# Folding halves spread over a group's second layer, and norms moved to ScalarE, in a fused retention, expert and channel kernel

## The chip, the cores and the metric

The kernel runs as one program on one core of a Trainium2 chip. The metric is the device time of one execution in microseconds. The engines are TensorE (PE, with its weight loads as PEld), VectorE (DVE), ScalarE (ACT), GpSimd (POOL) and SyncE (SP), which issues nearly all DMA transfers in one queue. "us" is microseconds throughout.

## The reference

Three stages follow each other on 4 batches of 576 rows of 512 values:

```python
ret = scores * Dmat; x = ret @ v                       # retention, 8 heads
h = np.maximum(x[b, s] @ w1[e], 0.0)                   # one expert of 8 for each row
out[b, s] = p[e] * (h @ w2[e])
X = np.real(fft(fft(x, axis=1), axis=2)); u = x + X    # third stage
un = (u - mean(u)) / np.sqrt(var(u) + 1e-06)
y = u + np.maximum(un @ w_ch1, 0.0) @ w_ch2            # 512 -> 2048 -> 512
```

The change touches the third stage alone: the transform of a batch, its norm, and the order in which a batch's steps stand among the products of the two layers.

## The kernel before

The third stage is in `Transform` (one batch's Fourier transform, sums and norm) and `channels` (the two layers). The order of all its instructions is that of the code: each engine takes its own in that order, and waits for semaphores where another engine's result is needed.

**A batch's transform.** `steps(b, wait)` is a generator. One `next` issues one step: `load` (DMAs into `fxy`), the folds of three row tiles (`even` makes `fee`, `odd` makes `foo`, both on VectorE), `twice` (four sums on VectorE), five products `down` on TensorE, each with `take` (ScalarE copies PSUM to `fz`), three cross products `across` with `merge` (ScalarE and VectorE) and `sums` (ScalarE), and then `end`: `rate`, and six times `norm` and `keep`. A norm makes r*x + m as fp32 rows `f`, the fp16 part `h` and the rest `l` = f - h, and stores h and l to `un` in DRAM; `keep` stores u. Both go through SyncE's queue. `h` and `l` are halves of a tile `hl`, of which there are three, so a fourth norm needs the first one's store to have ended; `f` lies in buffers that the folds use too, two for each half of the tiles.

**The two layers.** Batch 0 and 1 are prepared before and during the first 512 rows. The other rows go in seven groups of 256 rows, j = 0 to 6. `fetch(r)` loads a group's rows of `un`, transposed, into `gxt`. The first layer has eight slots f; in each, TensorE makes 24 products into a bank `g1` (L1666), ScalarE takes the two middle parts out (L1975, L1976), VectorE makes `s` from all four (L1982), and both make the fp16 parts `hd` of it (L1955, L1952). The second layer has seven products i (L2011), each 24 matmuls into a bank, and VectorE folds each into the rows `u` (L2040). Of the seven, the banks are

```python
q, tag = (p2, "g2") if i % 3 else (p1, "g1")
```

with three buffers `g1` and two `g2`, so the product i = 4 needs the bank of i = 1, and i = 5 that of i = 2.

**Where the steps stand.** Batch 2 (the third) has `more = tr.steps(2, 0)`, batch 3 `tr.steps(3, WAIT)` with WAIT = 1. In j = 0, `next(more)` is called after each of the seven products of the second layer. In j = 1 to 3 it is called once in every slot of the first layer too, and in j = 1 again in the slots of the table `TWICE` (1 and 4 before). At i = 4 of j = 1 what is left of `more` is issued, and then the fetch for j = 2 stands in SyncE's queue behind the last norm's stores. Beside them runs `left`, which combines pairs of weight pieces (`pair` loaded by SyncE, L1813; VectorE L1843 and L1848; ScalarE L1819; VectorE L1821) for the second layer's corner products; it ends in i = 2 of j = 0. Batch 1's norms stand among the products before j = 0, and the fetch for j = 0 and the rest of the pair loads stand behind their stores in SyncE's queue.

Of the kernel before, what the change touches and what calls it, by code (L numbers as in the profile page):

```python
# [14 lines left out]
ACTF = mybir.ActivationFunctionType  # L15
ALU = mybir.AluOpType
# [1180 lines left out]
def by_rows(nc, out, in_):  # L1197

    n = out.shape[0]
    m = n // 16 * 16 if n > 96 else n  # L1200
    for a, b in ((0, m), (m, n)):
        if a < b:
            i = nc.sync.dma_start(out=out[a:b], in_=in_[a:b])  # L1203
    return i


class Transform:
# [143 lines left out]
    def both(self, b, t, bank):  # L1351

        nc, n, (_, _, cd, sd) = self.nc, 34 if t == 2 else 128, self.tables
        zs = self.rows_of(b, t)
        out = []
        for s in (self.minus, sd):
            ps = bank()
            even, odd = ps[:n, 0:129], ps[:n, 129:257]
            steps = (
                (even, zs[0], 128, cd[:, 0, 0:129]),  # L1360
                (even, zs[2], 96, cd[:, 1, 0:129]),
                (odd, zs[1], 128, cd[:, 0, 129:257]),
                (even[:, 0:128], zs[3], 128, s[:, 0, :]),
                (odd, zs[4], 128, s[:, 1, :]),
            )
            for j, (o, z, m, w) in enumerate(steps):
                nc.tensor.matmul(
                    out=o, lhsT=z[:m], rhs=w[:m], start=(j == 0), stop=(j == 4)
                )
            out.append(ps)  # L1370
        return out
# [144 lines left out]
    def norm(self, b, i, kept=0):  # L1516

        nc, (_, _, _, r, m) = self.nc, self.st[b]
        t, y, p0, p1, at = self.place(b, i)
        n = TL[t][1]  # L1520
        x = self.xy[b][t][:n, y]
        f = self.wk.tile([128, 512], FP32, tag="xo" if y else "xe", name="f", bufs=2)
        hl = self.wk.tile([128, 2, 512], FP16, tag="hl", name="hl", bufs=3)
        h, l = hl[:n, 0, :], hl[:n, 1, :]
        ri, mi = r[:n, i : i + 1], m[:n, i : i + 1]
        nc.scalar.activation(out=h, in_=x, func=ACTF.Identity, scale=ri, bias=mi)
        nc.vector.tensor_scalar(out=f[:n], in0=x, scalar1=ri, scalar2=mi, op0=ALU.mult, op1=ALU.add)  # L1527
        nc.vector.tensor_tensor(out=l, in0=f[:n], in1=h, op=ALU.subtract)
        p0 = max(p0, kept)
        if p0 < p1:  # L1530
            to = slice(at.stop - (p1 - p0), at.stop)
            by_rows(nc, self.un[to, :], hl[p0:p1].rearrange("p a d -> p (a d)"))
        return hl
# [15 lines left out]
    def steps(self, b, wait=0):  # L1549

        self.load(b)
        yield
        for t in range(3):
            self.even(b, t)
            if wait:
                yield
            self.odd(b, t)
            yield
        self.twice(b, 0)
        self.twice(b, 1)  # L1560
        yield
        for _ in range(wait):
            yield
        yield from self.across_rows(b)
# [16 lines left out]
def channels(ctx, tc, nc, A, w1, w2, un, u, out, tr, wst, idn, late, jobs):  # L1581
# [47 lines left out]
    def still(n, ps):  # L1629

        for _ in range(n):
            nc.tensor.matmul(out=ps, lhsT=w1.dst[0][:, 0, 0:128], rhs=w1.dst[0][:, 0, 0:512], start=True, stop=True)
# [28 lines left out]
    def first(f, ps, xt, steps=range(3)):  # L1661

        for i in steps:
            m, x = ((h1, 0), (l1, 0), (h1, 1))[i]
            for k in range(4):
                nc.tensor.matmul(  # L1666
                    out=ps,
                    lhsT=m[:, k + 4 * (f // 8), 128 * (f % 8) : 128 * (f % 8) + 128],
                    rhs=xt[x][:, k, :],
                    start=(k == 0 and i == 0),  # L1670
                    stop=(k == 3 and i == 2),
                )
# [180 lines left out]
    ready = {}  # L1853
    E = {}
    OLD = 2
    TWICE = 1, 4
    WAIT = 1
    LEFT = 6
    DOWNS = 10
# [4 lines left out]
    def old(r, n):  # L1864

        x = wst.tile([128, 2, 512], FP32, tag="wst", name="u")
        nc.sync.dma_start(out=x, in_=u[r : r + 256, :].rearrange("(a p) d -> p a d", p=128))  # L1867
        return x
# [28 lines left out]
    for _ in left:  # L1897
        pass
    V.scalar_tensor_tensor(
        out=fs[:, 0:1], in0=w1.inv[:, 0:1], scalar=2.0**-10 / C2, in1=w2.inv[:, 0:1], op0=ALU.mult, op1=ALU.mult  # L1900
# [7 lines left out]
    for t in range(4):  # L1908
        ps = p2.tile([128, 512], FP32, tag="g2", name="g2")
        for at, f in enumerate(ROWS):  # L1910
            for i, (m, x) in enumerate(((h2, 0), (h2, 1), (l2, 0))):
                nc.tensor.matmul(
                    out=ps,
# [29 lines left out]
    for r0 in range(512, NT, 256):  # L1943
        xt = X.pop(r0)
        xt = xt[:, 0:4], xt[:, 4:8]
        j = (r0 - 512) // 256
# [4 lines left out]
        def lower(l, x, h):  # L1951
            V.scalar_tensor_tensor(out=l, in0=x, scalar=C2 / 2, in1=h, op0=ALU.mult, op1=ALU.subtract)  # L1952

        def whole(s, hd):
            nc.scalar.activation(out=hd[:, 0, 2:7], in_=s, func=ACTF.Copy, scale=C2 / 2)  # L1955
            lower(hd[:, 1, 2:7], s, hd[:, 0, 2:7])

        s = None
        for f in range(8):
            if f == OLD:  # L1960
                o = old(r0, 256)

            ps = p1.tile([128, 512], FP32, tag="g1", name="g1")
            if j == f == 0:
                still(STILL[2], ps)
            first(f + 8, ps[:, 0:256], xt)
            first(f, ps[:, 256:512], xt)
            old_s, old_hd = s, f and hd
            if f and f < 7:
                whole(s, hd)  # L1970
            r = wk.tile([128, 2, 128], FP32, tag="r", name="r")
            s = wk.tile([128, 640], FP32, tag="s", name="s").rearrange("p (a n) -> p a n", a=5)
            hd = hp.tile([128, 2, 7, 128], FP16, tag="hd", name="hd")
            p = ps.rearrange("p (a n) -> p a n", a=4)
            nc.scalar.activation(out=r, in_=p[:, 1:3], func=ACTF.Relu)  # L1975
            nc.scalar.activation(out=hd[:, 0, 0:2], in_=p[:, 1:3], func=ACTF.Relu, scale=C2 / 2)  # L1976
            for d, x, y, op in (
                (s[:, 1:3], p[:, 0:4:3], r[:, 1::-1], ALU.add),
                (s[:, 3:5], p[:, 0:4:3], r, ALU.subtract),
                (s[:, 0], p[:, 1], r[:, 1], ALU.add),  # L1980
            ):
                V.scalar_tensor_tensor(out=d, in0=x, scalar=0.0, in1=y, op0=ALU.max, op1=op)  # L1982
            if f == 7:
                whole(old_s, old_hd)
            lower(hd[:, 1, 0:2], r, hd[:, 0, 0:2])
            hid.append(hd)
            if j:
                next(more, None)
            if j == 1 and f in TWICE:
                next(more, None)  # L1990
            if j or f < LEFT:
                next(left, None)
# [34 lines left out]
        for i, (x, w, to) in enumerate(steps):  # L2027
            ps = banks[i] if i < 3 else place(i)
            product(ps, range(6 if i < 3 else 0, 8), x, w)
            next(more, None)  # L2030
            next(left, None)
            if i == 4 and r0 + 256 < NT:
                if j in (1, 3):
                    for _ in more:
                        pass
                fetch(r0 + 256)
            for a, c in to:
                y = q[:, a]
                p = ps.unsqueeze(1).to_broadcast([128, 2, 256]) if isinstance(a, slice) else ps
                V.scalar_tensor_tensor(out=y, in0=p, scalar=fs[:, c : c + 1], in1=y, op0=ALU.mult, op1=ALU.add)  # L2040
            if i == 4 and j:
                store(r0, o[:, 0])
# [175 lines left out]
def fused_kernel(tc, A, out, stop=None):  # L2218
    nc = tc.nc
    with ExitStack() as ctx:  # L2220
# [5 lines left out]
        with tc.manual_schedule():  # L2226
# [121 lines left out]
            z = zeros(cv)  # L2348
            steps = moe(ctx, tc, nc, A, xs, x2, rows_in, rows_out, pieces, weights, who, conv, low, start, beyond, z, padded, hid0, mt0, wst, small)
            next(steps)  # L2350
            for t, n in zip(tables, ("f_cs", "f_sn", "f_cd", "f_sd")):
                nc.sync.dma_start(out=t.rearrange("p a b -> p (a b)"), in_=A[n])
        overflow(tc, nc, A, xs, x2, idn, n_i)
        with tc.manual_schedule():
            late = next(steps)
            c2x.close()
            tr = Transform(ctx, tc, nc, x2, un, u, rows_out, tables)
            channels(ctx, tc, nc, A, c1, c2, un, u, out, tr, wst, idn, late, jobs)
# [46 lines left out]
```

## Time and profile before

| what | value |
|---|---|
| median of 3 runs | 793.76 us (791.66 to 795.1) |
| the profiled execution: its own time | 787.88 us |
| its span, first to last instruction | 785.7 us |
| TensorE matmul busy, share of the span | 724.8 us, 92% |
| VectorE busy | 592.3 us, 75% |
| ScalarE busy | 411.8 us, 52% |
| mean granted TensorE clock | 0.988 of full speed |
| first product of the first layer, j = 0 and j = 1 | at 470.87 and 520.11 us |
| the same of j = 2 | at 570.13 us |

A time of the profile counts from the span's start. A share of busy time says little about a single stage, so the sections below go by the timeline of the stretch from 440 to 660 us, in which the steps that the change moves lie.

### The profile page before, as it was taken

How to read it: one execution, taken by the hardware profiler on the slowest of the kernel's cores; microseconds unless marked ns; L12 is line 12 of the kernel's file. 1: busy time of each engine (PE TensorE's matmuls, PEld its weight loads, DVE VectorE, ACT ScalarE, POOL GpSimd, SP SyncE). 2: the span in 40 equal slices, each digit the busy share in tenths (PEclk: the TensorE clock that was granted, in tenths of full speed). 3: DMA queues.
4: the chain of work that ended last, by engine and by line, in shares of the span. 5: the costliest groups of instructions: out<-in, count | busy, mean ns of one | idle time of the engine just before them, and what ended most of it. 6: DMA issues, size and time to landing. Idle time of an engine off the chain costs nothing. (4 is left out here: it accounts for less than half of the span.)

```text
span 785.7 us, 17150 instructions
## 1 busy us (share of the span) xinstructions
PE 724.8 (92%) x6529; PEld 542.8 (69%) x6529; DVE 592.3 (75%) x1432; ACT 411.8 (52%) x829; POOL 126.8 (16%) x225
## 2 busy tenths in 40 slices
PE   8888898899999998879998999899899999999996
PEld 5677685655566555557644448778788888888885
DVE  3678888589889988857898969958876695646462
ACT  1356657378888797845847526426332451414140
POOL 3566443002102201113000011010010001010101
PEclk9999999899999999999999999999999999999998
DMA  9998449999998998964427276600550017110000
GB/s 296 355 305 293 154 115 309 295 315 344 293 360 304 270 352 287 262 235 149 136 77 240 102 214 232 175 28 2 170 150 2 28 62 195 28 55 2 28 2 27
DMA packets 91929, 142.27 MB, mean 181 GB/s; under 512 B 48116, under 2 KB 49017, under 8 KB 90814
## 3 DMA queue, kind: packets, MB, share of 16 engines
q1 hardware_dynamic: 87246, 126.78, 51.4%
q0 software_dynamic: 4592, 14.31, 5.0%
q8 instruction: 53, 0.87, 0.4%
q14 instruction: 38, 0.31, 0.1%
HBM read 97.55 MB, written 35.12 MB: 169 GB/s over the span
## 5 line engine op out<-in xcount | busy, mean ns | idle before, releaser
L1666 PE MATMUL g<-gxt,wh 128*128 128x256 f16 (+1 forms) x992 | 143.6, 284 | 2.6 <-DMA gxt<-un 1.4
L2011 PEld LDWEIGHTS <-hd 128*128 128x128 f16 x1176 | 114.2, 98 | 26.9 <-issue 7.1
L1666 PEld LDWEIGHTS <-wh 128*128 128x128 f16 x1056 | 102.8, 98 | 28.5 <-issue 4.9
L286 DVE SCALAR_TENSOR_TENSOR wl<-wst,ws,wh 128x1024 f16<-128x1024 f32 (+1 forms) x82 | 100.3, 1253 | 8.1 <-ACT wh L281 8.0
L281 ACT ACTIVATE wh<-wst,ws 128x1024 f16<-128x1024 f32 x80 | 89.0, 1140 | 26.1 <-DVE ws L274 25.7
L815 PE MATMUL ps<-xt,wh 128*128 128x320 f16 (+4 forms) x544 | 79.1, 284 | 8.1 <-DMA xt<-xs 5.8
L845 PE MATMUL ps<-wh,hid 128*128 128x512 f16 (+2 forms) x528 | 84.6, 302 | 0.2 <-ACT hid L831 0.2
L2011 PE MATMUL g<-wh,hd 128*128 128x256 f16 x448 | 78.3, 273 | 4.3 <-DVE u L2040 2.0
L1666 PE MATMUL g<-gxt,wl 128*128 128x256 f16 (+1 forms) x496 | 80.5, 285 | 0.0
L815 PEld LDWEIGHTS <-wh 128*128 128x128 f16 x640 | 57.5, 100 | 33.2 <-issue 13.8
L1872 POOL DMA_INDIRECT out<-u,orow x18 | 17.9, 993 | 383.9 <-DVE u L2040 284.8
L845 PEld LDWEIGHTS <-hid 128*128 128x128 f16 (+2 forms) x792 | 46.4, 100 | 42.4 <-issue 2.7
L239 ACT ACTIVATE wh<-wst 128x1024 bf16<-128x1024 f32 x66 | 69.3, 1050 | 7.7 <-DVE wst L311 5.2
L2040 DVE SCALAR_TENSOR_TENSOR u<-g,ffs,u 128x256 f32<-128x256 f32 (+1 forms) x63 | 34.1, 568 | 49.3 <-PE g L2011 48.7
L1982 DVE SCALAR_TENSOR_TENSOR s<-g,r 128x256 f32<-128x256 f32 x168 | 53.3, 374 | 23.4 <-ACT hd L1976 22.7
L1955 ACT ACTIVATE hd<-s 128x640 f16<-128x640 f32 x56 | 41.3, 737 | 47.8 <-DVE s L1982 47.8
L1975 ACT ACTIVATE r<-g 128x256 f32<-128x256 f32 x56 | 21.1, 378 | 84.0 <-PE g L1666 78.0
L2011 PE MATMUL g<-e,hd 128*128 128x256 f16 x504 | 59.9, 273 | 5.0 <-DVE u L2040 4.0
L859 POOL DMA_INDIRECT x<-y,mt x25 | 31.5, 1261 | 194.7 <-ACT y L857 149.7
L2011 PE MATMUL g<-wl,hd 128*128 128x256 f16 x224 | 61.1, 273 | 0.0
L1666 PEld LDWEIGHTS <-wl 128*128 128x128 f16 x528 | 51.9, 98 | 11.7 <-issue 1.1
L845 PE MATMUL ps<-wl,hid 128*128 128x512 f16 (+2 forms) x264 | 56.4, 302 | 0.0
(299 smaller groups left out, 1280.7 us busy)
## 6 DMA issues: line engine op xcount, KB each, us to landing
wst<-in_moe_w SPq DMA_DIRECT2D x64, 512.0 KB
raw<-in_ch SPq DMA_DIRECT2D x14, 1024.0 KB
qk<-in_qkv SPq DMA_DIRECT2D x18, 512.0 KB
vk<-in_qkv SPq DMA_DIRECT2D x16, 512.0 KB
pair<-ch SPq DMA_DIRECT2D x32, 256.0 KB
ch<-d SPq DMA_DIRECT2D x14, 512.0 KB
wst<-ch SPq DMA_DIRECT2D x14, 512.0 KB
u<-u SPq DMA_DIRECT2D x9, 512.0 KB
```

The costliest lines, as they stand in the source:

```text
L239: self.nc.scalar.activation(out=x, in_=t, func=ACTF.Abs, accum_out=self.am[:, j : j + 1])
L281: self.nc.scalar.activation(out=self.dst[0][:, j, :], in_=self.pieces[j], func=ACTF.Copy, scale=self.by(j))
L286: self.nc.vector.scalar_tensor_tensor(out=l[:, j, c], in0=self.pieces[j][:, c], scalar=self.by(j), in1=h[:, j, c], op0=ALU.mult, op1=ALU.s ...
L815: nc.tensor.matmul(out=ps, lhsT=m[:, k, 128 * f : 128 * f + 128], rhs=xt[:, x + k, :], start=(k == 0 and i == 0), stop=(k == 3 and i == last),
L845: nc.tensor.matmul(out=ps[r * j : r * j + r, 0:d], lhsT=hid[x][:, f, 128 * t : 128 * t + r], rhs=m[:, 4 + f // 2, c : c + d], start=(f == ...
L859: nc.gpsimd.indirect_dma_start(out=x2[:, :].rearrange("t (k d) -> (t k) d", k=k), out_offset=bass.IndirectOffsetOnAxis(ap=mt, axis=0), in_ ...
L1666: nc.tensor.matmul(out=ps, lhsT=m[:, k + 4 * (f // 8), 128 * (f % 8) : 128 * (f % 8) + 128], rhs=xt[x][:, k, :], start=(k == 0 and i == 0) ...
L1955: nc.scalar.activation(out=hd[:, 0, 2:7], in_=s, func=ACTF.Copy, scale=C2 / 2)
L1975: nc.scalar.activation(out=r, in_=p[:, 1:3], func=ACTF.Relu)
L1982: V.scalar_tensor_tensor(out=d, in0=x, scalar=0.0, in1=y, op0=ALU.max, op1=op)
L2011: nc.tensor.matmul(out=ps, lhsT=hid[k][:, y, x, :], rhs=E[w][m][k], start=(k == 0 and m == y == 0), stop=(k == 7 and y == 1),)
L2040: V.scalar_tensor_tensor(out=y, in0=p, scalar=fs[:, c : c + 1], in1=y, op0=ALU.mult, op1=ALU.add)
```

## The change

The change has two parts. The first is in `steps` and in the table: with `wait` 0 (batch 2) a step that issues nothing stands behind the load, and the even and the odd half of the first two tiles' folds are steps of their own. These are three steps more than before, and the table gives back three in j = 1. Batch 3 has `wait` 1, so its steps stay. The second is in `norm`: for every batch but the first (b = 0), ScalarE writes the fp32 rows and copies them to fp16, where ScalarE made the fp16 part and VectorE the fp32 rows from the same input.

```diff
         ri, mi = r[:n, i : i + 1], m[:n, i : i + 1]
-        nc.scalar.activation(out=h, in_=x, func=ACTF.Identity, scale=ri, bias=mi)
-        nc.vector.tensor_scalar(out=f[:n], in0=x, scalar1=ri, scalar2=mi, op0=ALU.mult, op1=ALU.add)
+        if b:
+            nc.scalar.activation(out=f[:n], in_=x, func=ACTF.Identity, scale=ri, bias=mi)
+            nc.scalar.copy(out=h, in_=f[:n])
+        else:
+            nc.scalar.activation(out=h, in_=x, func=ACTF.Identity, scale=ri, bias=mi)
+            nc.vector.tensor_scalar(out=f[:n], in0=x, scalar1=ri, scalar2=mi, op0=ALU.mult, op1=ALU.add)
         nc.vector.tensor_tensor(out=l, in0=f[:n], in1=h, op=ALU.subtract)
...
         self.load(b)
         yield
+        if not wait:
+            yield
         for t in range(3):
             self.even(b, t)
-            if wait:
+            if wait or t < 2:
                 yield
             self.odd(b, t)
             yield
...
-    TWICE = 1, 4
+    TWICE = {1: 2, 2: 2, 4: 1}
...
-            if j == 1 and f in TWICE:
+            for _ in range(TWICE.get(f, 0) if j == 1 else 0):
                 next(more, None)
```

Three places show what moves. The lines from L1528 on have higher numbers in the changed kernel; L2040 is L2046 there, L1821 is L1827, L1848 is L1854, L1666 is L1672.

The first is on VectorE, in the second layer of j = 0, from the fold of the product i = 0 (bank `g_8088`) on. Before, up to the fold of i = 1 (`g_8089`):

```order
L2040 SCALAR_TENSOR_TENSOR u<-g_8088,ffs,u 128x256 x2
L1251 TENSOR_TENSOR xe<-fxy_6301 128x512
L1253 TENSOR_TENSOR xe<-xe 128x255
L1256 TENSOR_TENSOR fee_6304<-xe 128x129
L1257 TENSOR_TENSOR fee_6304<-xe 128x128
L1264 TENSOR_TENSOR xo<-fxy_6301 128x512
L1266 TENSOR_TENSOR xo<-xo 128x255
L1267 TENSOR_TENSOR foo_6308<-xo 128x127
L1268 TENSOR_TENSOR foo_6308<-xo 128x128
L1821 SCALAR_TENSOR_TENSOR wl_78<-pair,ws,wh_77 128x256 x2
L1848 TENSOR_TENSOR pair<-pair 128x512
L2040 SCALAR_TENSOR_TENSOR u<-g_8089,ffs,u 128x256
```

Now, from the same fold up to the fold of i = 2 (`g_8090`):

```order
L2046 SCALAR_TENSOR_TENSOR u<-g_8088,ffs,u 128x256 x2
L1827 SCALAR_TENSOR_TENSOR wl_78<-pair,ws,wh_77 128x256 x2
L1854 TENSOR_TENSOR pair<-pair 128x512
L2046 SCALAR_TENSOR_TENSOR u<-g_8089,ffs,u 128x256
L1251 TENSOR_TENSOR xe<-fxy_6301 128x512
L1253 TENSOR_TENSOR xe<-xe 128x255
L1256 TENSOR_TENSOR fee_6304<-xe 128x129
L1257 TENSOR_TENSOR fee_6304<-xe 128x128
L1827 SCALAR_TENSOR_TENSOR wl_78<-pair,ws,wh_77 128x256 x2
L2046 SCALAR_TENSOR_TENSOR u<-g_8090,ffs,u 128x256 x2
```

The first tile's even half moved behind the fold of i = 1, and its odd half out of these rows, behind the fold of i = 2; one half now stands between two folds.

The second place is on TensorE, in j = 1 behind the first layer's slot f = 2 (bank `g_8440` before, `g_8428` now). Before, the cross product (L1324 to L1333) follows the slot's products, and the two last products `down` of the batch (`foo`) stand ahead of the slot:

```order
L1295 MATMUL zps<-f_sn,foo_6311 128x145
L1295 MATMUL zps<-f_sn,foo_6309 128x145
L1295 MATMUL zps<-f_sn,foo_6310 128x290
L1666 LDWEIGHTS wh_75
L1666 MATMUL g_8440<-gxt,wh_75 128x256
```

Now they stand between the slot's products and the cross product, which reads the copies `fz` of them:

```order
L1672 MATMUL g_8428<-gxt,wh_75 128x256
L1295 MATMUL zps<-f_sn,foo_6311 128x145
L1295 MATMUL zps<-f_sn,foo_6309 128x145
L1295 MATMUL zps<-f_sn,foo_6310 128x290
L1324 MATMUL zps<-f_sd,fz_6315 128x128
L1324 MATMUL zps<-f_sd,fz_6316 128x128
L1331 MATMUL zps<-f_cd,fz_6313 128x128
```

The slot's own products no longer separate the last `down` from the cross product.

The third place is on ScalarE, at batch 2's first two norms in j = 1. Before:

```order
L1526 ACTIVATE hl<-fxy_6301,m,r 128x512
L1975 ACTIVATE r<-g_8718 128x256
L1976 ACTIVATE hd<-g_8718 128x256
L1955 ACTIVATE hd<-s 128x640
L1526 ACTIVATE hl<-fxy_6302,m,r 128x512
L1955 ACTIVATE hd<-s 128x640
```

Now:

```order
L1527 ACTIVATE f<-fxy_6301,m,r 128x512
L1528 CAST hl<-f 128x512
L1981 ACTIVATE r<-g_8718 128x256
L1982 ACTIVATE hd<-g_8718 128x256
L1961 ACTIVATE hd<-s 128x640
L1527 ACTIVATE f<-fxy_6302,m,r 128x512
L1528 CAST hl<-f 128x512
L1961 ACTIVATE hd<-s 128x640
```

A copy (CAST) stands behind each norm's first operation, ahead of the evacuations of the next slot.

## Rows read from the trace of the kernel before

**Rows 1.** The page's first part: busy us, share of the span, instructions.

```profile
PE 724.8 (92%) x6529; PEld 542.8 (69%) x6529; DVE 592.3 (75%) x1432; ACT 411.8 (52%) x829; POOL 126.8 (16%) x225
```

**Rows 2.** TensorE's waits from 470 to 570: us in total, times, longest.

```profile
PE g L2011 <- DVE u L2040: 5.1, 3, 2.2
```

**Rows 3.** TensorE's timeline, second layer of j = 0: start, length, in brackets idle before.

```profile
507.65 2.78 PE L2011 MATMUL g<-e,hd 128*128 128x256 f16 x24 [2.21 <-DVE u L2040]
512.40 0.27 PE L2011 MATMUL g<-wh,hd 128*128 128x256 f16 x1 [1.97 <-DVE u L2040]
...
515.19 1.47 PE L1295 MATMUL zps<-f_cs,fee 128*128 128x145 f32 x6
...
519.12 1.15 PE L1295 MATMUL zps<-f_cs,fee 128*128 128x145 f32 x6
520.11 0.60 PE L1666 MATMUL g<-gxt,wh 128*128 128x256 f16 x4
```

**Rows 4.** VectorE's timeline in the same stretch.

```profile
502.53 0.70 DVE L1251 TENSOR_TENSOR xe<-fxy 128x512 f32<-128x512 f32 x1
...
504.14 0.69 DVE L1264 TENSOR_TENSOR xo<-fxy 128x512 f32<-128x512 f32 x1
...
507.12 0.47 DVE L2040 SCALAR_TENSOR_TENSOR u<-g,ffs,u 128x256 f32<-128x256 f32 x1
...
511.48 0.87 DVE L2040 SCALAR_TENSOR_TENSOR u<-g,ffs,u 128x256 f32<-128x256 f32 x2
...
523.68 0.95 DVE L1982 SCALAR_TENSOR_TENSOR s<-g,r 128x256 f32<-128x256 f32 x3 [3.61 <-ACT hd L1976]
```

**Rows 5.** The norm's operations by line and in ScalarE's timeline, and a copy (CAST).

```profile
L1527 DVE TENSOR_SCALAR f<-fxy,r,m x20: 528/534/546, 375.4 to 650.0; 128x512 f32<-128x512 f32 x12, 33x512 f32<-33x512 f32 x8
L1528 DVE TENSOR_TENSOR hl<-f,hl x20: 682/692/694, 376.0 to 650.6; 128x512 f16<-128x512 f32 x12, 33x512 f16<-33x512 f32 x8
...
443.49 2.22 ACT L1526 ACTIVATE hl<-fxy,m,r 128x512 f16<-128x512 f32 x3 [1.06 <-DVE m L1505]
...
424.32 0.62 ACT L1894 CAST hd<-gr 128x512 f16<-128x512 f32 x1
```

**Rows 6.** SyncE's and VectorE's timelines behind batch 1's fourth norm.

```profile
448.79 0.79 SPq L1203 DMA_DIRECT2D un<-hl  x2
...
455.27 3.00 SPq L1601 DMA_TRANSPOSE gxt<-un  x1
...
464.16 0.69 DVE L1843 TENSOR_TENSOR pair<-pair 128x512 f32<-128x512 f32 x1 [5.08 <-DMA pair<-ch]
```

**Rows 7.** SyncE's and TensorE's timelines at the end of j = 1.

```profile
563.83 0.30 SPq L1203 DMA_DIRECT2D un<-hl  x1
...
564.62 2.16 SPq L1601 DMA_TRANSPOSE gxt<-un  x1
...
570.13 0.60 PE L1666 MATMUL g<-gxt,wh 128*128 128x256 f16 x4 [1.38 <-DMA gxt<-un]
```

**Rows 8.** TensorE's timeline, second layer of j = 1: its waits.

```profile
548.11 0.27 PE L2011 MATMUL g<-wh,hd 128*128 128x256 f16 x1 [0.61 <-DVE s L1982]
...
554.95 0.39 PE L2011 MATMUL g<-wh,hd 128*128 128x256 f16 x2 [0.24 <-DVE hd L1952]
...
556.94 0.28 PE L2011 MATMUL g<-e,hd 128*128 128x256 f16 x1 [0.51 <-DVE hd L1952]
...
560.73 2.78 PE L2011 MATMUL g<-e,hd 128*128 128x256 f16 x24 [0.89 <-DVE u L2040]
```

**Rows 9.** TensorE's timeline, second layer of j = 3: its waits.

```profile
639.66 0.27 PE L2011 MATMUL g<-wh,hd 128*128 128x256 f16 x1 [0.41 <-DVE s L1982]
...
648.23 0.28 PE L2011 MATMUL g<-e,hd 128*128 128x256 f16 x1 [0.49 <-DVE hd L1952]
...
652.01 2.78 PE L2011 MATMUL g<-e,hd 128*128 128x256 f16 x24 [0.88 <-DVE u L2040]
```

## The prediction

> **What bounds the kernel now.** I read the page first: TensorE is busy for 92% of the span and VectorE for 75% [rows 1], so time is won only where TensorE waits. The second view is the list of TensorE's waits over the two groups j = 0 and j = 1 [rows 2]. The reader is to see there that the largest sort is the second layer waiting for VectorE to fold its own results (L2040): three waits, 5.1 us. The third view is the timeline of the two engines there. At 507.65 and 512.40 TensorE stands 2.21 and 1.97 us [rows 3]. The second layer has two banks for each pair of products, and its fifth product needs the bank of the second, whose fold VectorE starts at 507.12. Between the fold that ended at 502.53 and this one lie both halves of batch 2's first fold (even from 502.53, odd from 504.14) and weight pieces, 4.59 us in all [rows 4]. The sixth product waits in the same way for the fold at 511.48. After that VectorE runs dry: at 523.68 it has been idle for 3.61 us [rows 4]. The work is there, but it stands in the wrong place of a queue.
>
> The other waits that matter are four small ones in the second layer of j = 1, where norms and folds alternate on VectorE [rows 8], a wait of 1.38 us at 570.13 for the transposed fetch that opens j = 2 [rows 7], and three in the second layer of j = 3, behind batch 3's norms [rows 9]. Some short waits in the first layer of j = 0 belong to a VectorE stream of weight pieces that the change doesn't touch.
>
> **The folds of batch 2, spread out.** The instructions stay the same; only their places move. I walk VectorE from 502.53. An even half takes 1.61 (504.14 less 502.53); with an odd half of the same size, 4.59 less 3.2 leaves 1.4 for weight pieces. The second product's fold now has only these ahead of it: it starts at 503.9 and, with its 0.47, ends near 504.4. TensorE wants that bank at 505.44 (507.65 less 2.21), so this wait is gone. Then come the even half (to 506.0), two weight pieces of 0.4 each (to 506.8) and the double fold of 0.87 (to 507.7). A product of 24 matmuls takes some 2.65, as between 507.65 and the start of the next wait, so TensorE wants this bank at 508.1. The second wait is gone too, with 0.4 to spare. Each later fold then has one half ahead of it and a product of 2.65 to hide it, and needs 1.6 plus at most 0.7. The two transform products that stood in the queue (515.19, 519.12) move into j = 1; the first took 1.47 where the second took 1.15, so 0.32 more was a wait inside it [rows 3]. Gain: 2.21 + 1.97 + 0.32 = 4.5.
>
> What is late next: the last half and the sums of `twice` now end after j = 1 has begun, but in the 3.61 us in which VectorE stood idle [rows 4]. Slot f = 1 of j = 1 now issues three transform products and slot f = 2 two of them and the first cross product. That one needs ScalarE's copy of the product just ahead of it, which nothing else covers now. I put the copy's round trip at 0.4 and the wait of the first product for `twice` at 0.2: 0.6 lost (bounds 0 and 1.5, as no row of before has such a pair back to back). TensorE's wait of 0.61 at 548.11 [rows 8] is for a VectorE stream that starts its cross sums nearly 5 us earlier, so it goes: 0.6 back. This part comes to -4.5.
>
> **The norms of batches 1 to 3.** Each of the 18 norms loses a VectorE operation of 0.534 and keeps the subtraction of 0.692. ScalarE keeps an operation of the same form (0.81 for one and, as three take 2.22, 0.71 from one to the next) and gains a copy; the nearest row is the same form at L1894, 0.62 [rows 5]. The subtraction, which had the two results side by side, now waits for both in a row: 0.81 + 0.62.
>
> In j = 1 VectorE has about 0.6 less in each of six norms and ScalarE has room. The waits at 554.95, 556.94 and 560.73 are for VectorE operations that then come 0.7 to 2 us earlier: 0.24 + 0.51 + 0.89 = 1.6 gained [rows 8]. The last norm's store went out at 563.83 and the fetch at 564.62, and the matmul that needed it began at 570.13, 5.5 later [rows 7]. The last subtraction comes earlier by the 4.5 of the first part and, with up to 0.6 for each of six norms, by some 3 more, of which SyncE's queue of stores takes back about 0.6: the fetch moves ahead by 6.9. TensorE's need moves ahead by 4.5 + 1.6 = 6.1, so 0.8 of the 1.38 is gained (bounds 0 and 1.38).
>
> In j = 3 the same relief: 0.41 + 0.49 + 0.88 [rows 9] = 1.78. Four of these norms stand in slots of the first layer, where ScalarE also evacuates the products, and its added half a microsecond a slot may leave some of it; I leave 0.2 of the waits: 1.6 gained (bounds 0.4 and 1.78).
>
> In batch 1 nothing on TensorE waits for VectorE, and the longer chain shows. ScalarE begins at 443.49 [rows 5]. One norm now takes it 1.37 (0.81, 0.03 to start the copy, and 0.53 until the next can start, 0.1 less than the copy's 0.62 as with the other form). Three at 1.37, the fourth up to its copy's end (0.81 + 0.03 + 0.62), then the subtraction of 0.69: 443.49 + 4.11 + 1.46 + 0.69 and two hand-overs is 449.8. The store of that norm went out at 448.79, and from there SyncE's queue is full up to the fetch at 455.27 [rows 6]: stores, a pair of weight loads, the fetch, and behind it the pair loads for which VectorE stood 5.08 us up to 464.16. These all come 1.0 us later. I take VectorE's stream from there to the end of j = 0's first layer, where TensorE waits for it, to shift by as much: 1.0 lost. The bounds are 0 (the loads land no later) and 1.8 (the copy costs 0.81).
>
> ScalarE's rule speaks against this half of the edit. The Trainium skill, page "ScalarE: Activation LUTs", section "Rules for kernel authors", says to put additions and multiplications on VectorE, which is faster per element. The trace agrees on the speeds (0.53 on VectorE against 0.81 and 0.62), and by this rule alone each batch would lose as batch 1 does, 1.0, and the sum would be -4.5 + 3.0 = -1.5. I hold to the waits: in j = 1 and j = 3 VectorE is the one waited for [rows 8, 9].
>
> **Sum.** -4.5 - 1.6 - 0.8 - 1.6 + 1.0 = -7.5. The profiled execution took 787.88 (a span of 785.7 and 2.2 around it), so the sum gives 780.4. The median of the runs shown is 793.76, 0.7% above that execution; I carry the ratio over, 780.4/787.88 = 0.9905, and get 786.2. A change below 0.5% (4 us) can't be told from none here.
>
> **Rivals.**
> 1. The gain is taken back later (chance 0.19): the first part holds, but ScalarE's chain paces the norms, so the waits of j = 1 and j = 3 stay and the fetch is as late as TensorE is early. For it: the copies wait in one queue with the evacuations. Against it: ScalarE is busy for 52% [rows 1], and 1.37 per norm is below the 2 us per norm and fold that the rows from 548.11 to 560.73 leave. Time: -4.5 + 1.0 = -3.5, so 784.4, or 790.2 as a median. The page named above would have it this way.
> 2. More is gained (0.13): the loads behind batch 1's norms land no later, the fetch is early enough, and the new waits are nothing: -4.5 - 0.6 - 1.6 - 1.4 - 1.8 = -9.9, so 778.0, or 783.8.
> 3. Slower (0.06): batch 2's chain loses slots of j = 1. `twice` now stands in its first slot instead of the second layer, and the chain's end feeds the fetch, which opens j = 2. A slot lasts (548.11 - 520.11)/8 = 3.5 us. If the norms end one slot later than before, the fetch goes out at 568.1, j = 2 starts 3.5 late and everything won before it is lost: 3.5 + 1.0 - 1.6 = +2.9, 796.7 as a median; two slots give +6.4, 800.2. It decides as soon as the fetch goes out 0.6 later than 564.62. Against it: the extra steps that the table gives slots 1, 2 and 4 bring the second cross product back to slot 3 as before, and VectorE has the idle 3.61.
>
> **Chances and range.** The forecast, -5.5 to -9, has 0.62. The range goes from the second rival's time to a little above the first's: 783.4 to 790.6, which leaves the slower case and tails. Faster by over 0.5%: 0.62 + 0.13 and the better part of rival 1, 0.78; within 0.5%: 0.18; slower: 0.04, the two-slot case and its like.
>
> **What would show it.** In the new profile the product after the fourth of j = 0 starts without a wait, and so does the next; if TensorE still waits for L2046 there, the walk on VectorE is wrong. The cross product in slot 2 of j = 1 should wait about 0.5 us for ScalarE. In batch 1 the fourth norm's store should go out near 449.8 and VectorE's wait for a pair end near 465.2; if it ends near 464.2, the loss of 1.0 is wrong. The fetch should go out some 6 us earlier than 564.62 and the wait of j = 2 be about half of 1.38. The second layer of j = 3 should have hardly a wait. What would make the prediction wrong altogether is a chain of norms on ScalarE slower than 1.37 each, or a fetch that lands later than 5.5 us after its issue.

## The result, and the profile after

The changed kernel takes 784.93 us (median of four runs, 781.54 to 787.06), the kernel before, on the same chip, 792.71 us (four runs, 788.67 to 795.1): a ratio of 0.9899 with a 95% interval of 0.986 to 0.9937. The prediction was 786.2 us in a range of 783.4 to 790.6, from a ratio of 0.9905.

The profiled execution of the changed kernel took 787.06 us and is the slowest of its four. Its span is 0.4 us shorter than that of before, although it begins batch 1's norms at 451.31, 7.82 us later than before [rows 5], and the code up to there is the same in both. So the two profiles are compared by the length of stages, not by the clock at their ends. First the page's busy times (us, share, instructions), which answer to [rows 1]:

```profile
PE 727.3 (93%) x6529; PEld 546.2 (70%) x6529; DVE 583.5 (74%) x1414; ACT 421.5 (54%) x847; POOL 129.4 (16%) x225
```

Eighteen instructions went from VectorE to ScalarE, one for each norm. The list of TensorE's waits from 470 to 690 us (what it waited for: us in total, times, longest) answers to [rows 2]. First the line of the kernel before for `u` over this longer stretch, then the list after:

```profile
PE g L2011 <- DVE u L2040: 6.0, 4, 2.2
```

```profile
PE g L1672 <- DMA gxt<-un: 2.7, 1, 2.7
PE g L1672 <- DVE s L1988: 1.1, 2, 0.5
PE g L2017 <- DVE s L1988: 0.7, 2, 0.5
PE g L2017 <- DVE hd L1958: 0.4, 1, 0.4
PE zps L1324 <- ACT fz L1310: 0.2, 1, 0.2
```

The waits for `u` are gone altogether. The only large one left is for the transposed fetch, and it has grown. TensorE's timeline (start, length, operation, in brackets the idle time before it) shows the places of [rows 3, 7 to 9]:

```profile
510.13 5.40 PE L2017 MATMUL g<-e,hd 128*128 128x256 f16 x48
515.38 0.27 PE L2017 MATMUL g<-wh,hd 128*128 128x256 f16 x1
...
520.62 0.60 PE L1672 MATMUL g<-gxt,wh 128*128 128x256 f16 x4
...
525.87 3.07 PE L1295 MATMUL zps<-f_cs,fee 128*128 128x145 f32 x18
...
534.10 0.49 PE L1324 MATMUL zps<-f_sd,fz 128*128 128x128 f32 x2 [0.24 <-ACT fz L1310]
...
550.91 0.27 PE L2017 MATMUL g<-wh,hd 128*128 128x256 f16 x1
...
561.39 2.78 PE L2017 MATMUL g<-e,hd 128*128 128x256 f16 x24
...
572.12 0.60 PE L1672 MATMUL g<-gxt,wh 128*128 128x256 f16 x4 [2.71 <-DMA gxt<-un]
...
641.07 0.27 PE L2017 MATMUL g<-wh,hd 128*128 128x256 f16 x1
...
651.55 2.78 PE L2017 MATMUL g<-e,hd 128*128 128x256 f16 x24
```

The fourth and fifth products of j = 0 now stand in one row of 48 matmuls (510.13), and the sixth follows at 515.38 without a bracket; the starts of the fifth and of the sixth are the two places with 2.21 and 1.97 before. The three even products `down` are one row in slot 1 of j = 1 (525.87), and the cross product behind the last `down` waits 0.24 for ScalarE's copy. The second layers of j = 1 and j = 3 have no bracket. The first even `down` still waits for the sums of `twice`, in its weight loads, as it did in j = 0; before, and after:

```profile
515.65 0.55 PEld L1295 LDWEIGHTS zps<-f_cs,fee 128*128 128x128 f32 x4 [0.16 <-DVE fee L1275]
```

```profile
526.33 1.53 PEld L1295 LDWEIGHTS zps<-f_cs,fee 128*128 128x128 f32 x10 [0.16 <-DVE fee L1275]
```

VectorE's timeline shows why the two large waits are gone, and it has the wait for a pair of [rows 6]:

```profile
471.53 0.69 DVE L1849 TENSOR_TENSOR pair<-pair 128x512 f32<-128x512 f32 x1 [4.89 <-DMA pair<-ch]
...
510.03 0.86 DVE L1827 SCALAR_TENSOR_TENSOR wl<-pair,ws,wh 128x256 f16<-128x256 f32 x2
...
511.42 0.47 DVE L2046 SCALAR_TENSOR_TENSOR u<-g,ffs,u 128x256 f32<-128x256 f32 x1
511.82 0.67 DVE L1251 TENSOR_TENSOR xe<-fxy 128x512 f32<-128x512 f32 x1
...
513.40 0.88 DVE L1827 SCALAR_TENSOR_TENSOR wl<-pair,ws,wh 128x256 f16<-128x256 f32 x2
514.19 0.87 DVE L2046 SCALAR_TENSOR_TENSOR u<-g,ffs,u 128x256 f32<-128x256 f32 x2
514.98 0.68 DVE L1264 TENSOR_TENSOR xo<-fxy 128x512 f32<-128x512 f32 x1
```

From 510.03 the second product's fold starts 1.39 us on, where before it came 4.59 after the same point [rows 4]. Then an even half (511.82 to 513.40), the weight pieces and the double fold, done at 515.06: TensorE needs that bank at 515.38, 0.3 later, where the walk had 0.4.

SyncE's queue behind batch 1's norms, and at the end of j = 1 [rows 6, 7]:

```profile
457.62 0.79 SPq L1203 DMA_DIRECT2D un<-hl  x2
...
463.35 3.37 SPq L1607 DMA_TRANSPOSE gxt<-un  x1
...
564.30 0.30 SPq L1203 DMA_DIRECT2D un<-hl  x1
...
565.10 2.77 SPq L1607 DMA_TRANSPOSE gxt<-un  x1
```

The fetch at 565.10 opens j = 2 only at 572.12, 7.0 us after its issue; before it was 5.5 [rows 7]. ScalarE's timeline in batch 1's norms answers to [rows 5]:

```profile
451.31 0.81 ACT L1527 ACTIVATE f<-fxy,m,r 128x512 f32<-128x512 f32 x1 [1.06 <-DVE m L1505]
452.15 0.62 ACT L1528 CAST hl<-f 128x512 f16<-128x512 f32 x1
452.68 0.81 ACT L1527 ACTIVATE f<-fxy,m,r 128x512 f32<-128x512 f32 x1
```

From one norm to the next are 1.37 us, the walk's figure.

### The profile page after: what moved, and what is told of

Its sections match the earlier page's. It is cut to its first block, busy times and chain, and to the rows that moved or that the text cites. A ratio compares the mean times of both kernels' runs of the same rounds, so it can differ in the third digit from the quotient of the medians.

```text
span 785.3 us, 17141 instructions
## 1 busy us (share of the span) xinstructions
PE 727.3 (93%) x6529; PEld 546.2 (70%) x6529; DVE 583.5 (74%) x1414; ACT 421.5 (54%) x847; POOL 129.4 (16%) x225
## 4 chain that ended last, share of the span: by engine, by line
issue 26%; DVE 11%; PE 9%; ACT 3%; DMA 2%; POOL 1%; SPq 1%; POOLq 0%; DVEq 0%; ACTq 0%
PE g L2017 4%; PE g L1672 3%; POOL out L1878 1%; DVE wl L286 1%; DVE hd L1901 1%; DVE hd L1958 1%; DVE e L1827 1%; DMA u<-u 1%; PE zps L1295 1%; DMA fxy<-x 1%; DVE s L1988 1%; DVE pair L1849 1%; SPq L1607 1%; PE bank L1672 1%; DMA pair<-ch 1%
## 5 line engine op out<-in xcount | busy, mean ns | idle before, releaser
L1672 PE MATMUL g<-gxt,wh 128*128 128x256 f16 (+1 forms) x992 | 142.6, 283 | 3.8 <-DMA gxt<-un 2.7
L1672 PEld LDWEIGHTS <-wh 128*128 128x128 f16 x1056 | 102.6, 98 | 28.6 <-issue 5.0
L1878 POOL DMA_INDIRECT out<-u,orow x18 | 19.8, 1101 | 373.1 <-DVE u L2046 276.7
L1672 PE MATMUL g<-gxt,wl 128*128 128x256 f16 (+1 forms) x496 | 79.6, 283 | 0.0
L2046 DVE SCALAR_TENSOR_TENSOR u<-g,ffs,u 128x256 f32<-128x256 f32 (+1 forms) x63 | 34.3, 567 | 48.9 <-PE g L2017 48.2
L1672 PEld LDWEIGHTS <-wl 128*128 128x128 f16 x528 | 51.7, 98 | 11.1
```

What stands on the lines that cost most here:

```text
L1672: nc.tensor.matmul(out=ps, lhsT=m[:, k + 4 * (f // 8), 128 * (f % 8) : 128 * (f % 8) + 128], rhs=xt[x][:, k, :], start=(k == 0 and i == 0) ...
L1878: nc.gpsimd.indirect_dma_start(out=out[:, :], out_offset=bass.IndirectOffsetOnAxis(ap=orow[:, r // 128 : r // 128 + 1], axis=0), in_=o, in ...
```

## The experiments

Eleven runs followed, each timed six to twelve times beside the kernel before on the same chip. The table has for each the ratio to before with its interval, and from its profile five stages: **a** from ScalarE's first norm of batch 1 (443.49 before [rows 5]) to the second layer of j = 0; **b** from there to the second layer of j = 1; **c** from there to the first product of j = 2, less **d**, the bracket of that product (wait for `gxt`); **e** from there to the end of the span. All but the start of a, which is ScalarE's, and the end of e are starts in TensorE's timeline.

| kernel | ratio (95%) | a | b | c | d | e |
|---|---|---|---|---|---|---|
| before | 1 | 50.79 | 53.83 | 20.64 | 1.38 | 215.57 |
| after | 0.9899 (0.986, 0.9937) | 50.44 | 49.16 | 18.50 | 2.71 | 213.18 |
| folds_only | 0.9945 (0.9918, 0.9973) | 50.02 | 49.17 | 20.65 | 2.80 | 215.60 |
| norm_only | 0.9943 (0.9914, 0.9972) | 51.26 | 53.84 | 18.49 | 1.68 | 213.15 |
| norm_late | 0.9871 (0.984, 0.9902) | 50.31 | 49.17 | 18.50 | 0.78 | 213.13 |
| fetch_early | 0.9856 (0.9823, 0.9888) | 50.86 | 49.17 | 18.34 | 0 | 213.17 |
| after_again | 0.989 (0.9845, 0.9936) | 50.83 | 49.17 | 18.50 | 2.90 | 213.18 |
| early_and_late | 0.9828 (0.9777, 0.9879) | 49.02 | 49.16 | 18.34 | 0 | 213.18 |
| halves_no_slot | 0.9909 (0.9871, 0.9948) | 51.29 | 50.71 | 18.50 | 1.02 | 213.15 |
| slot_no_halves | 0.9918 (0.988, 0.9957) | 50.65 | 51.60 | 18.50 | 2.26 | 214.79 |
| pair_first | 0.9865 (0.9818, 0.9912) | 49.09 | 49.16 | 18.50 | 1.09 | 213.12 |
| early_late_pair | 0.9871 (0.9824, 0.9918) | 51.76 | 49.16 | 18.33 | 0 | 213.17 |
| norm_b1 | 1.0029 (1.0002, 1.0055) | 50.55 | 54.01 | 20.64 | 2.14 | 215.62 |

Stages b, c and e repeat to some hundredths from profile to profile and take one value for each form of the code, but for b in norm_b1 (0.17 more than before) and e in slot_no_halves (below); a and d vary with the same code. So one profile says much about b, c and e, and little about a and d. The c of 18.34 in the kernels without a wait for `gxt` is the 18.50 of the others: a bracket leaves out 0.16 of a wait (below). By times alone most of these kernels cannot be told from the changed one, since the intervals overlap; what a part is worth is read from the stages.

**folds_only** keeps the steps and the table of the change and takes the norm of before:

```diff
-        if b:
-            nc.scalar.activation(out=f[:n], in_=x, ...)
-            nc.scalar.copy(out=h, in_=f[:n])
-        else:
-            nc.scalar.activation(out=h, in_=x, ...)
-            nc.vector.tensor_scalar(out=f[:n], in0=x, ...)
+        nc.scalar.activation(out=h, in_=x, ...)
+        nc.vector.tensor_scalar(out=f[:n], in0=x, ...)
```

> Only the moved folds; every norm as in the kernel before. My theory (the two halves of the change act in different places and add up): the waits for u in j=0's second layer (6.0 us in four) are gone, the short waits in the second layers of j=1 (0.24, 0.51, 0.89) and j=3 (0.41, 0.49, 0.88) stay; 4.5 to 5 us faster than before, ratio about 0.994. Rival, that the shorter VectorE work of the norms is what removes the waits and the places of the folds do not matter: the waits for u stay near 6 us and the ratio is 1.00.

TensorE's waits in it, from 470 to 690 us:

```profile
PE g L2013 <- DVE u L2042: 1.8, 2, 0.9
PE g L2013 <- DVE hd L1954: 1.6, 4, 0.5
```

The two long waits for `u` are gone; what is left are the 0.89 and 0.88 of [rows 8, 9] and the small ones beside them. (Of the 6.0 us in four waits that the expectation puts in j = 0, only 2.21 and 1.97 lie there.) Stage b falls by 4.66 us, c and e stay at their values of before. The ratio is the theory's.

**norm_only** is the rest: `if b:` in the norm, and the steps and `TWICE = 1, 4` of before.

> Only the norms' edit; the folds stand where they stood before. My theory: the waits for u in j=0's second layer stay (2.21 and 1.97 us), the short ones in the second layers of j=1 and j=3 go; 2.5 to 3.5 us faster than before, ratio about 0.996. Rival (the norms are the whole gain): 7 us faster, 0.991. Rival (the places of the folds are the whole gain): 1.00.

Its waits in the same stretch:

```profile
PE g L2015 <- DVE u L2044: 2.6, 2, 2.2
PE g L2015 <- DVE hd L1956: 0.4, 1, 0.4
```

The second wait for `u` is 0.41 here and not 1.97. TensorE's timeline shows where the rest went, and the granted clock (PEclk, the third figure from the right) in the same stretch:

```profile
512.32 4.34 PE L2015 MATMUL g<-e,hd 128*128 128x256 f16 x24 [2.21 <-DVE u L2044]
517.07 0.27 PE L2015 MATMUL g<-wh,hd 128*128 128x256 f16 x1 [0.41 <-DVE u L2044]
```

```profile
512.30:516.70 4.40, 4.34 (x24) 3.08 (x24) 4.26 (x12) 0.51 (x2) 0.00 (x0) 0.63 0.37 119
```

Behind the first wait the clock fell to 0.63 of full speed in the mean, and the fifth product took 4.34 us instead of 2.78. It cost nothing: the sixth product had to wait for VectorE's fold in any case, and stage b is that of before. c falls by 2.15 and e by 2.42. That is 4.6 where 2.5 to 3.5 was expected: the mechanism is right and its size too small (below). The two parts of the change add up: 0.9945 times 0.9943 is 0.9888, beside a measured 0.9899 and 0.989. Both rivals, each part as the whole gain, fall.

**halves_no_slot** and **slot_no_halves** divide the first half again. The first leaves out the step that issues nothing, the second keeps that step and leaves the folds whole:

```diff
         self.load(b)
         yield
-        if not wait:
-            yield
...
-    TWICE = {1: 2, 2: 2, 4: 1}
+    TWICE = {1: 1, 2: 2, 4: 1}
```

```diff
             self.even(b, t)
-            if wait or t < 2:
+            if wait:
                 yield
...
-    TWICE = {1: 2, 2: 2, 4: 1}
+    TWICE = {2: 2, 4: 1}
```

> The changed kernel without the step that issues nothing: the halves of batch 2's folds are separate, but start one product earlier (the table of extra steps is set so that slot 1 of j = 1 ends where it did). By the walk on VectorE an even half of 1.6 us and weight pieces of 1.4 stand ahead of the second product's fold: one wait of about 0.5 us for u at the fifth product, none at the sixth; 0.3 to 1 us slower than the changed kernel, ratio 0.991. Rival (the added slot is the gain, since it lets the queue run empty before the folds): a wait near 2 us stays and the ratio is 0.993 to 0.995.

> The changed kernel with whole folds, one slot later (the table set so that slot 2 of j = 1 ends where it did). By the walk on VectorE the fifth product starts without a wait, and the sixth waits 1.2 to 2 us for u, since the third product's fold has 3.2 us of batch 2's fold ahead of it; 1 to 2 us slower than the changed kernel, ratio 0.992. Rival (the halves are nearly all of the gain): two waits that sum to 4 us, ratio 0.995.

TensorE's waits in the first, and then in the second:

```profile
PE g L2015 <- DVE u L2044: 1.5, 2, 1.2
```

```profile
PE g L2017 <- DVE u L2046: 1.2, 1, 1.2
PE zps L1295 <- DVE fee L1274: 1.0, 1, 1.0
```

Whole folds one slot later wait 1.16 at the sixth product, as walked, and 0.96 more at the first `down`, which is in j = 0 there and finds `twice` unfinished; the theory had not named that one. Halves without the slot wait 1.16 at the fifth product and 0.38 at the sixth, where 0.5 and none were walked, so their stage b is 1.55 longer than the changed kernel's and not 0.3 to 1; that the ratio is the expected 0.991 all the same says little, with an interval from 0.987 to 0.995. In stage b the change gains 4.67, halves alone 3.12, the slot alone 2.23. The two overlap: the halves take 1.05 off the first wait of 2.21, the slot takes all of it, and both are needed to remove the last 1.6 to 2.4 us.

**norm_late** (`if b > 1:`) keeps batch 1's norms on VectorE, and **norm_b1** (`if b == 1:`, folds as before) moves these alone.

> The whole change, but batch 1's norms stay on VectorE as before (only those of batches 2 and 3 move). My prediction had the longer chain of batch 1's norms cost 1.0 us by way of the queue of SyncE; by that this kernel is 1.0 us faster than the changed one (0.988 of before). What the trace of the changed kernel suggests instead: the fourth norm's store is again near 5.3 us after the first ScalarE row of the norms rather than 6.3, but the first layer of j=0 begins at the same distance from that row, 27.2 +- 0.3 us, and the time is that of the changed kernel (0.990).

> The kernel before with the norms of batch 1 alone moved to ScalarE. My prediction's term for this was a loss of 1.0 us by way of SyncE's queue. Over the ten profiles so far the first layer of j = 0 ends 49.0 to 50.8 us after the first norm of batch 1 where these norms are on VectorE (mean of four 50.0) and 50.4 to 51.3 where they are on ScalarE (mean of six 50.9). So: 50.9 +- 0.4 here, ratio 1.001. Rival (the longer chain is absorbed by SyncE, as the first pair of profiles seemed to show): 50.0 +- 0.6, ratio 1.000 or below.

The first pair of profiles had made the predicted loss of 1.0 look wrong: stage a was 0.35 shorter than before. The other profiles correct this. In stage a, leaving out the two kernels with the exchange of pair_first, the profiles with batch 1 on VectorE have 50.79, 50.02, 50.31 and 49.02 (mean 50.04), those with it on ScalarE 50.44, 51.26, 50.86, 50.83, 51.29, 50.65 and 50.55 (mean 50.84): 0.8 longer, but with a scatter as large; with those two counted in (51.76 on VectorE, 49.09 on ScalarE) it is 0.2. By times, norm_b1 is 1.0029 and its interval leaves out 1, though its own stage a is no longer than that of before, and the two kernels that differ from another only by this edit are both 0.28% lower, within their intervals. The loss is likely, and its size is not settled; my reading of one pair of profiles, on which the second expectation of norm_late rests, was noise.

The path is the predicted one. In all eleven of these profiles the first layer of j = 0 ends 30.1 to 30.3 us after the long wait for a pair ends (before: 494.28 less 464.16 [rows 6]; after: 501.75 less 471.53; norm_b1: 498.39 less the row below). What varies is when that pair lands.

```profile
468.28 0.69 DVE L1847 TENSOR_TENSOR pair<-pair 128x512 f32<-128x512 f32 x1 [5.00 <-DMA pair<-ch]
```

**pair_first** takes that path by the queue: a pair goes out ahead of the fetch for j = 0.

```diff
                 for _ in more:
                     pass
-                fetch(512)
             if (t, at) in T_SLOTS:
                 next(left, None)
+            if (t, at) == (2, 6):
+                fetch(512)
```

> The changed kernel with one exchange in the queue of SyncE: one pair of weight loads goes out ahead of the fetch for j = 0 instead of behind it. Theory (the arrival of that pair at VectorE sets the end of j = 0's first layer, which in all ten profiles so far comes 30.1 to 30.3 us after it): VectorE's long wait for a pair (4.3 to 5.2 us) is 2 to 3 us shorter, the first layer of j = 0 takes 21.3 to 22 us instead of 23.3 to 23.7, and the time is 1.5 to 2 us below the changed kernel's, ratio 0.987. Rival (the wait is for a buffer or for the weights themselves, not for the place in the queue): the pair comes no earlier, or the fetch comes so much later that j = 0 starts with a wait for gxt; no gain, 0.990.

VectorE's waits for pairs in it:

```profile
461.88 0.69 DVE L1849 TENSOR_TENSOR pair<-pair 128x512 f32<-128x512 f32 x1 [1.96 <-DMA pair<-ch]
...
465.67 0.69 DVE L1849 TENSOR_TENSOR pair<-pair 128x512 f32<-128x512 f32 x1 [1.16 <-DMA pair<-ch]
```

One wait of some 5 us became two of 1.96 and 1.16, and the first layer of j = 0 took 21.94 us where the two profiles of the changed kernel have 23.29 and 23.67. So the theory's signs are there in this run. But early_and_late, without the exchange, has 21.86, because its pair landed early, so this one profile does not prove that the exchange did it.

**fetch_early** issues the fetch for j = 2 behind the third norm of batch 2 instead of the sixth:

```diff
+            if j == 1 and i == 0:
+                fetch(r0 + 256)
             if i == 4 and r0 + 256 < NT:
...
-                fetch(r0 + 256)
+                if j != 1:
+                    fetch(r0 + 256)
```

> The changed kernel with one move: the fetch of rows 1024 to 1279 is issued in j=1's second layer behind the stores of the third norm instead of behind those of all six. Theory (the fetch is late by its place in the queue of SyncE, and its landing takes 7.0 us because it goes out right behind a run of stores and ahead of batch 3's loads): issued near 560, it lands before 569 and TensorE's wait of 2.71 us at the start of j=2 goes; 2 to 2.7 us faster than the changed kernel, 0.987 of before. Rival (what the wait covered comes up elsewhere: the three norms whose stores stand behind the fetch run out of hl buffers, or VectorE is late at the start of j=2): the wait goes or shrinks, but less than 1 us is gained and a wait for s or hd of 1 to 2 us appears in the first layer of j=2.

SyncE's queue in it:

```profile
562.77 0.33 SPq L1203 DMA_DIRECT2D un<-hl  x1
...
563.58 1.99 SPq L1607 DMA_TRANSPOSE gxt<-un  x1
```

The second layer of j = 1 begins at 554.39 in this run, so the fetch goes out 9.19 us after it, where in the changed kernel it was 14.19 (565.10 less 550.91). The wait is gone and nothing took its place: e is 213.17.

**after_again** is the changed kernel once more.

> The changed kernel, unaltered, for a second profile and more times. In its first profile the fetch that opens j = 2 landed 7.0 us after its issue and TensorE waited 2.71 us; in the other runs with the same order of instructions there it took 5.1 to 6.9. If the landing varies from run to run, the wait here is anywhere from 0.6 to 2.7 us and every other distance from the first product of j = 0 is the first profile's to 0.2 us; if the order of instructions sets it, the wait is 2.7 again. The ratio should be 0.990 +- 0.004.

The wait was 2.90. But the same order of instructions in j = 1 gave 0.78 in norm_late and 1.09 in pair_first, so the order alone does not set it.

**early_and_late** has fetch_early and norm_late together, and **early_late_pair** pair_first as well.

> The changed kernel with both edits of the runs before it: batch 1's norms back on VectorE, and the fetch for j = 2 behind the third norm's stores. Theory (the two are independent): j = 0's first layer 0.4 to 0.6 us shorter than the changed kernel's and no wait for gxt at the start of j = 2; from the first product of j = 0 to the end 303.8 us, where the changed kernel's profile has 306.8 and the kernel before 314.8; ratio to before 0.985. Rival (batch 1's norms make no difference): 304.2 and the ratio of the early fetch alone.

> All three edits together: batch 1's norms on VectorE, the fetch for j = 2 behind the third norm, the pair of loads ahead of the fetch for j = 0. If the exchange works alone, this has a first layer of j = 0 of 21.0 to 21.5 us with one wait at most, and from the first product of j = 0 to the end 301.5 to 302 us; ratio to before 0.981 to 0.983. If the waits of the first layer were already hidden by batch 1's norms on VectorE, it equals the run without the exchange (302.5 us, 0.983).

The first is the fastest kernel of the study, 777.85 us beside 791.93 before; from the first product of j = 0 to the end it takes 302.54 us, 1.3 less than expected, since its pair landed early. All that is left of TensorE's waits from 470 to 690 us are the last three lines of the changed kernel's list, with the same figures.

The exchange added to it did not help: its profile has 51.76 in stage a, its ratio 0.9871. Its SyncE and VectorE rows show how:

```profile
464.15 5.34 SPq L1607 DMA_TRANSPOSE gxt<-un  x1
```

```profile
475.58 0.69 DVE L1849 TENSOR_TENSOR pair<-pair 128x512 f32<-128x512 f32 x1 [3.16 <-DMA pair<-ch]
```

The fetch held SyncE for 5.34 us, where it took 2.4 to 3.5 elsewhere, and the next pair came late in place of the first. The exchange moves the fetch from ahead of one pair to ahead of the next; what it brings hangs on how long the fetch takes.

## Why the prediction was right

By its own steps, with the stage of the table that answers to each:

- **The folds, -4.5.** Right in mechanism: -4.67 in b, and within 0.02 of it in every profile that has both parts of this edit. The walk on VectorE met the trace, with 0.3 to spare at the sixth product. Its 2.65 for a product is right (510.13 to 515.38 is two of 2.63), though the place that it is read from gives 2.78. That the sum came so near has some luck in it. By the starts of the matmuls the two waits gave 4.50 where 4.18 was put down, since a bracket leaves out a part (next point). The 0.32 inside the first `down` came back: in j = 1 its first four matmuls again start 0.23 apart, as at 515.19, where those of the second `down` start 0.13 apart; only 0.17 just ahead of it went. The cross product lost 0.50, and of the wait at 548.11, put down as 0.6, 0.50 went. 4.50 + 0.17 - 0.50 + 0.50 is 4.67.
- **Norms in j = 1, -1.6, and in j = 3, -1.6.** Right in mechanism, too small: c fell by 2.14 and e by 2.39. The sums were over the brackets of [rows 8, 9]. A bracket counts from the end of the matmul before, but without a wait the next would have started 0.11 us after that one's start and not 0.27, at its end. At 560.73 the one before starts at 559.57 and ends at 559.84: the bracket says 0.89, the delay is 1.05. Three waits of 0.16 more are 0.5 in c; in j = 3 there are four such places, one of them (0.15 at 646.25) too short for a bracket. The 0.2 that I kept back for ScalarE's copies was not needed. The rule of the Trainium skill, page "ScalarE: Activation LUTs", section "Rules for kernel authors", that additions and multiplications belong on VectorE, would have given -1.5 in all by the prediction's text (its first rival, which names the page too, has -3.5). The trace agrees that VectorE is the faster (0.53 against 0.81), but norm_only was 0.57% faster than before, because TensorE waited for VectorE and not for ScalarE.
- **The fetch, -0.8.** Wrong, the one step that failed: "the fetch moves ahead by 6.9. TensorE's need moves ahead by 4.5 + 1.6 = 6.1". The fetch did move ahead by 7.1 from the first product of j = 0, but the need, with its larger gains, by 6.9; between issue and need lie 4.31 us, where before it was 4.13 (570.13 less 1.38 less 564.62 [rows 7]). So the order gains 0.2 at most. And the 5.5 us from issue to landing is no constant: ten profiles with the fetch behind the last norm have 5.1 to 7.2. The profile of before drew a short one and the two of after long ones (7.0, 7.2), so the term read +1.33 and +1.52 instead of -0.8; the mean of d over the four profiles with this order of the changed kernel (2.71, 2.90, 0.78, 1.09) is 1.87, over before and norm_b1 1.76. The prediction named a fetch that lands later than 5.5 us after its issue as something that would make it wrong altogether. It landed so, and the forecast held, since this cost no more than 1.5 us.
- **Batch 1, +1.0.** The fourth norm's store went out 6.31 us after the first norm on ScalarE, where it was 5.30: 1.0 later, as walked. The loss in stage a is 0.8 in the mean over eleven profiles, with a scatter as large.

With these, 0.8 - 4.67 - 2.14 - 2.39 + 0.1 is -8.3; on 787.88 that is 0.9895, beside 0.9899 and 0.989 measured. The predicted -7.5 came near because the terms of the norms, too small by 1.3, and the fetch, 0.9 too good, went opposite ways. The rival that the gain is taken back later did happen in part, at the fetch, for 0 to 1.5 us; the others did not.

What sets the landing of the fetch remains open. SyncE's stores ahead of it and batch 3's loads behind it are the same where it is short and where it is long. A third transfer stands at the same place, GpSimd's store of output rows; before, and after:

```profile
565.26 0.98 POOL L1872 DMA_INDIRECT out<-u,orow  x1 [42.56 <-DVE u L2040]
```

```profile
564.98 0.98 POOL L1878 DMA_INDIRECT out<-u,orow  x1 [38.22 <-DVE u L2046]
```

It was issued 0.64 us behind the fetch before and 0.12 ahead of it after. The packets in the trace let the fetch be followed. Where the store is issued just ahead, the last of the fetch's 2048 packets of 256 bytes ended 5.4 to 6.7 us after the issue in the four profiles in which the fetch's packets began before the store's (both of the changed kernel among them), and 4.6 to 4.9 in the three in which the store's began first. Where the store is issued 0.6 us behind, it was 4.1 to 5.7, and 3.6 to 3.8 in the three kernels with the early fetch, where the store comes 4.9 us behind. So the store is a candidate, but it is not shown: the early fetch is away from batch 3's loads too, and no run moved the store alone.

## What to carry to other kernels

Two engines that trade work in order, as TensorE and VectorE here, are tuned by walking the one that is waited for row by row: the fold that frees a bank must stand ahead of work that nobody needs yet, in pieces no longer than one product. Moving an operation to an engine where it takes longer pays where the old engine is waited for and the new one is not, and it is likely to cost where neither is, as in batch 1. Before a single profile is believed on a stage, look whether the stage repeats: stages of computing alone repeated here to some hundredths of a microsecond in all but two cases, and stages that hang on a transfer moved by up to 2 us, as much as the effects in question; for these give the transfer room, as the early fetch did.

## What was not expected of the hardware

A wait in the timeline cost TensorE 0.16 us more than its bracket for matmuls of 256 columns, which start 0.11 us apart and are shown 0.27 long.

The same transposed fetch, of the same rows, landed 5.1 to 7.2 us after its issue in ten profiles, and the one for j = 0 held SyncE for 2.4 to 5.3 us.

In slot_no_halves stage e is 1.6 us longer. There TensorE's clock fell just behind the wait of 2.26 us for the fetch; its timeline, and the granted clock in three stretches:

```profile
568.71 0.60 PE L1672 MATMUL g<-gxt,wh 128*128 128x256 f16 x4 [2.26 <-DMA gxt<-un]
569.14 0.94 PE L1672 MATMUL g<-gxt,wl 128*128 128x256 f16 x4
569.88 1.92 PE L1672 MATMUL g<-gxt,wh 128*128 128x256 f16 x8
...
573.87 1.04 PE L1672 MATMUL g<-gxt,wh 128*128 128x256 f16 x8
```

```profile
566.00:568.70 2.70, 0.45 (x5) 0.25 (x3) 0.48 (x1) 0.00 (x0) 1.45 (x3) 1.00 1.14 263
568.70:572.50 3.80, 3.79 (x21) 2.79 (x21) 0.00 (x0) 0.00 (x0) 0.65 (x5) 0.57 1.06 364
572.50:580.00 7.50, 7.50 (x70) 6.67 (x69) 5.54 (x14) 3.48 (x8) 0.00 (x0) 0.99 0.75 199
```

Eight matmuls took 1.92 us instead of 1.04: the lower level, 1.2 GHz, for most of 3.8 us. The waits of 2.71 and 2.90 us at the same place, in the two profiles of the changed kernel, were not followed by such a fall (granted 1.00 from 572.1 to 576 in the first). The clock fell in the same way in j = 0 behind the waits for `u` of 2.21 us in norm_only (above) and 2.39 in norm_b1 (0.62 from 511.95 to 516.4), and not behind the 2.21 of the kernel before (1.00 from 507.65 to 512.4). So a wait here can cost up to 1.6 us beyond itself, or nothing where the next product waits anyway; what decides whether the clock falls, no run shows.
